# Scoring four attention units in one visit, w_out in longer rows, and earlier q and k requests, in a fused sliding-window attention and gated feed-forward kernel

## The chip, the cores and the metric

The kernel runs on one core of a Trainium2 chip. A core has a matrix engine (TensorE, here PE, with its weight loads shown apart as PEld), a vector engine (VectorE, DVE), a scalar engine (ScalarE, ACT), a general engine (GpSimd, POOL) and a synchronising engine (SyncE, SP). Each runs its own instruction stream in order; streams wait for each other on semaphores. Sixteen DMA engines move data between the chip's memory and the on-chip memories. Matrix products land in PSUM, eight banks of 512 float32 values in each of 128 partitions. The metric is the time of one execution in microseconds (us).

## What is computed

Sliding-window attention with sinks, and a two-layer feed-forward with a gate behind it, cut to what matters:

```python
B, H, S, D = 4, 8, 768, 64
scores = q @ k.T / sqrt(D)                    # per batch and head
keep = (key < 4) | ((0 <= query - key) & (query - key < 128))
a = softmax(where(keep, scores, -1e9))
x = (a @ v).transpose(0, 2, 1, 3).reshape(3072, 512)
h = x @ w_in                                  # (512, 2048)
g = h * sigmoid(beta * h)                     # beta has one value per hidden column
out = g @ w_out                               # (2048, 512), float32 out
```

The products are made from bfloat16 operands and summed in float32.

## The kernel before

The 3,072 tokens are cut into NT = 8 tiles of TT = 384 (half a sequence). A **unit** is one head pair in one token tile: 8 tiles x 4 pairs = 32 units, numbered so that units 4T to 4T+3 make token tile T. A unit with half = 1 (second half of a sequence) also needs scores against the four sink keys.

A unit goes through these steps. *In*: PE transposes its q and k (`transpose_in`, L626) and DVE or ACT copies them to `qkT`. *Sink*, *a*, *b*: scores. *Av*: the product with v (`attend`, L745) and the normalising on DVE (`normalise`, L776). *Out*: PE transposes the result (`transpose_out`, L786) and DVE copies it to `xT`. Units from XBAR = 12 on have both transposes made by DMA instead, and are scored in one visit: `scores_at_once` (L717) fills all four score banks (s0, s1, "tr", "av"), with one exponential and one mask of 1,536 columns a partition. Units 4 to 11 are scored in two half visits (`scores`, L680: steps a and b), each with two banks, an exponential (L707) and a mask (L714) of 768 columns. In these units the bank "tr" takes the transposes, "av" the value products.

The feed-forward has a first product per **block**: a block is one of NM = 16 groups of 128 hidden columns for one token tile, four matmuls of 128x384 (L814, `hidden_matmul`), then ACT's tanh (L822) and DVE's gate (L835). Banks h0 and h1 take turns; in token tile 0 the two accumulators help. The second product (`project`, L841) has 48 matmuls of 128x512 a token tile (3 token rows of 128 by 16 hidden groups) in the accumulators acc0 and acc1. For token tile 0 the order is rows 0 and 1 in turn, one in each accumulator, then row 2; later tiles go row by row.

A main loop (L938) over steps s writes the program in its natural order: at s = 0 to 15 the blocks of token tile 0; then a **gap** of eight steps (16 to 23) without blocks, in which units 4 to 7 are done; then the blocks of the other tiles. The table `AGENDA` says in which step each unit does what (units 8 to 11 begin at steps 23, 26, 28 and 31), and `products(s)` (L70) how many products of the second kind a step takes: three in the gap, two at steps 24 and 25, one to step 39, three from step 40. From this list a planner in the kernel (`Prog.order`, L184) builds each engine's real order before anything runs: it walks the operations with estimated durations and transfer times, and on each engine takes the ready operation that can start first, the earlier in the program where two are equal, within a window of 200 operations. So the order on an engine is fixed when the kernel is built, and at run time an engine waits for its next instruction even if a later one could go.

Transfers: SP requests q and k of units 0 to 11 (float32, `load_qk`, L517); POOL casts them (L621), makes masks, and requests w_in (four transfers, L578), w_out (eight transfers of two groups, L583), v of later tiles, and from unit 12 on the q, k and v (L552, L561). POOL's requests convert to bfloat16 on the way. An `after` argument makes a request wait for an earlier transfer's landing: q and k of units 4 to 7 wait for w_in's second transfer, `("w_in", 0, 4)`; those of units 8 to 11 for one of w_out's.

w_out's group m holds rows 128m to 128m+127, one row a partition, so a transfer of two groups reads two rows of 2 KB for each partition. Accordingly block m uses the hidden columns 128m to 128m+127 of w_in, and beta, which is read as 16 rows of 128 and transposed by PE (L883), gets one column a block.

Of the kernel before, what the change touches and what calls it, by code (L numbers as in the profile page):

```python
# [11 lines left out]
DM, DF, NOUT = 512, 2048, 512  # L12
NTOK = B * S
# [31 lines left out]

NEG = -1.0e6
# [10 lines left out]
for n in range(4, 8):  # L57
    for step, at in (("in", n - 4), ("sink", 16), ("a", 16), ("b", 16), ("av", 17), ("out", 18)):
        AGENDA.setdefault(at if step == "in" else at + 1 * (n - 4), []).append((n, step))
# [10 lines left out]
def products(s):  # L70

    return 0 if s < NM else 3 if s < NM + GAP or s >= 2 * NM + GAP else 2 if s < NM + GAP + 2 else 1
# [284 lines left out]
def bass_streamingllm_window__then__act_swish_beta_kernel(  # L357
# [32 lines left out]
    beta_stage = sb("beta_stage", (16, 128), F32)  # L390
# [183 lines left out]
    w_out_src = moe_w_out.rearrange("(m p) n -> p m n", p=128)  # L574
# [7 lines left out]
    def load_w_out(m, ms, after=()):  # L582
        op("gp", lambda e: e.dma_start(w_out16[:, m:m + ms, :], w_out_src[:, m:m + ms, :]), after=after,  # L583
           w=[("w_out", mm) for mm in range(m, m + ms)],
           dma=f"wo{m}", **transfer(ms * 128 * NOUT * 4, 416, 740.0, 3.0))
# [39 lines left out]

    def transpose_in(n, eng="dve"):  # L626
        _, _, half, pb = place(n)
        bank16 = tr_ps[:, :].bitcast(BF16)
        z = n % NQK
        for which, name in enumerate("qk"):  # L630
            with P.together("pe"):
                for c in range(3):
                    at = (3 * which + c) * 128
                    op("pe", lambda e, which=which, c=c, at=at: nc.tensor.transpose(
                        bank16[:, at:at + 128],
                        qk16[z][:, which, c, :, :].rearrange("p h d -> p (h d)"), ident[:, :]),
                       r=[(name + "16", z), "ident"], w=["tr"], **pe(128))
# [3 lines left out]
        op(eng, lambda e: (e.copy if eng == "act" else e.tensor_copy)(dst, src),  # L641
           x=["tr"], w=[("qkT", pb, half)], **(act(768) if eng == "act" else dve(865.0)))
# [168 lines left out]
    def hidden_matmul(i, c):  # L811
        T, m = i // NM, i % NM
        bank, name = hidden_bank(i)
        op("pe", lambda e: e.matmul(  # L814
            bank, w_in16[:, c, m * 128:(m + 1) * 128], xT[:, c, T * TT:(T + 1) * TT],
            start=(c == 0), stop=(c == 3)),
           r=[("w_in", c, m), ("xT", T, c)], w=[name], **pe(TT))
# [46 lines left out]
    op("act", lambda e: e.dma_start(beta_stage[:, :], moe_beta.rearrange("(m p) -> m p", p=128)),  # L864
# [4 lines left out]
    for c in range(6):  # L869
# [13 lines left out]
    op("pe", lambda e: nc.tensor.transpose(acc[1][:, 0:16], beta_stage[:, :], ident32[0:16, 0:16]),  # L883
       r=["beta_stage", "ident32"], w=["acc1"], **pe(64))
    op("dve", lambda e: e.tensor_scalar(beta_half[:, :], acc[1][:, 0:16], 0.5, None, ALU.mult),
# [15 lines left out]
    for n in range(4):  # L901
# [36 lines left out]
    for s in range(-2, S_END + NM):  # L938
# [4 lines left out]
        for n, step in AGENDA.get(s, ()):  # L943
# [5 lines left out]
            if step == "b" and n >= XBAR:  # L949
                scores_at_once(n)  # L950
                later.append(lambda n=n: mask_at_once(n))
            if step in ("a", "b") and n < XBAR:
                c = "ab".index(step)
                if n < 8 and c == 1:
# [86 lines left out]
```

## Time and profile before

| | |
|---|---|
| median of three runs | 229.1 us (228.0 to 230.09) |
| profiled execution | 228.59 us |
| its span, first to last instruction | 226.9 us |
| instructions | 4,463 |
| HBM read, written | 27.34 MB, 6.29 MB |

The profile shows one execution. "Busy" is time in which an engine executes, not counting its requests; a share is of the span. For PE, busy includes the time that a matmul takes to run through the array, which overlaps the next one, so what a matmul costs in a dense stream is the distance to the next start. PEclk is the clock that PE was granted, 1.00 being full. The chain of waits is followed back from the last instruction: at each step to what released it, or to the instruction before it on its engine. A row with `<-` names what ended an idle time. q0 is the DMA queue of POOL's requests, q1 that of SP's, q10 that of ACT's. "To landing" is the time from a request's issue to the arrival of its last byte.

### The profile page before, as it was taken

The numbers are of one execution on the slowest core, as the hardware profiler recorded it, in microseconds if no ns is written. First come the engines' busy times: TensorE is split into PE (matmuls) and PEld (weight loads), VectorE is DVE, ScalarE is ACT, GpSimd is POOL, SyncE is SP. The second block draws the span as 40 slices with busy tenths as digits, with TensorE's granted clock in tenths as the row PEclk, the third lists the DMA queues.
The fourth block names the chain that finished last, engine by engine and source line by source line (L and its number), as shares of the span: only waits on it lengthen the run. The fifth ranks groups of instructions, "written<-read, shape, count | busy, mean of one in ns | idle before, by whom it ended". The sixth has DMA issues, their size and how long they took to land.

```text
span 226.9 us, 4463 instructions
## 1 busy us (share of the span) xinstructions
PE 220.0 (97%) x1761; PEld 122.1 (54%) x1761; DVE 132.6 (58%) x264; ACT 141.3 (62%) x224; POOL 125.7 (55%) x191
## 2 busy tenths in 40 slices
PE   7999989999999999999999999999999999999995
PEld 4665545555555555555555555555555555555454
DVE  5466777488975776566565656555656564443200
ACT  1877796197586877566657766666656755555311
POOL 4689992899994979695939396876300000000000
PEclk9999999999999999999999999999999999999999
DMA  6999999999998999999999999998921012110122
GB/s 172 251 172 179 276 194 205 257 228 139 118 138 124 124 117 151 120 167 144 116 113 135 99 138 147 96 165 119 94 80 53 20 57 64 49 46 0 58 83 92
DMA packets 96901, 28.92 MB, mean 127 GB/s; under 512 B 83424, under 2 KB 93936, under 8 KB 96880
## 3 DMA queue, kind: packets, MB, share of 16 engines
q0 software_dynamic: 59232, 10.92, 65.7%
q1 hardware_dynamic: 34304, 16.79, 34.3%
q10 hardware_dynamic: 3344, 0.93, 1.9%
q8 instruction: 14, 0.23, 0.5%
q14 instruction: 7, 0.06, 0.1%
HBM read 27.34 MB, written 6.29 MB: 148 GB/s over the span
## 4 chain that ended last, share of the span: by engine, by line
PE 73%; DMA 15%; POOL 8%; issue 2%; SPq 1%; ACT 0%; POOLq 0%; ACTq 0%
PE acc L843 32%; PE h_ps L814 29%; DMA k_stage<-in_k_dram 8%; DMA w_out<-in_moe_w_out_dram 4%; PE s_ps L727 4%; PE s_ps L770 4%; POOL qk L621 3%; DMA w_in<-in_moe_w_in_dram 2%; POOL land L552 2%; PE h_ps L843 2%; POOL v_aug L561 1%; PE s_ps L759 1%; PE s_ps L670 1%; SPq L522 1%; POOL v_aug L532 0%
## 5 line engine op out<-in xcount | busy, mean ns | idle before, releaser
L822 ACT ACTIVATE th<-h_ps,beta_half 128x384 f32<-128x384 f32 x120 | 69.4, 581 | 59.7 <-PE h_ps L814 59.1
L843 PE MATMUL acc<-w_out,g 128*128 128x512 bf16 x368 | 99.7, 380 | 0.0
L814 PE MATMUL h_ps<-xT,w_in 128*128 128x384 bf16 x480 | 96.2, 326 | 0.0
L835 DVE SCALAR_TENSOR_TENSOR g<-th,h_ps 128x384 bf16<-128x384 f32 x120 | 65.6, 550 | 44.8 <-ACT th L822 44.0
L814 PEld LDWEIGHTS h_ps<-xT,w_in 128*128 128x128 bf16 x480 | 45.6, 98 | 39.8 <-issue 0.8
L843 PEld LDWEIGHTS acc<-w_out,g 128*128 128x128 bf16 x368 | 32.8, 98 | 28.8 <-issue 3.6
L552 POOL DMA_DIRECT2D land<-in_q_dram x40 | 30.2, 760 | 24.0 <-DVE rden L779 24.0
L552 POOL DMA_DIRECT2D land<-in_k_dram x40 | 30.3, 761 | 0.0
L561 POOL DMA_DIRECT2D v_aug<-in_v_dram x40 | 30.2, 760 | 0.0
L735 ACT ACTIVATE E<-s_ps 128x1536 bf16<-128x1536 f32 x20 | 28.8, 1442 | 0.0
L741 DVE TENSOR_TENSOR E<-E,mask 128x1536 bf16<-128x1536 bf16 x20 | 19.2, 958 | 16.4 <-ACT E L735 16.4
L851 ACT ACTIVATE out_sb<-acc 128x512 f32<-128x512 f32 x23 | 13.7, 596 | 7.6 <-PE acc L843 7.4
L770 PEld LDWEIGHTS s_ps<-v_aug,E 128*128 128x128 bf16 x336 | 15.2, 97 | 3.2 <-issue 1.2
L770 PE MATMUL s_ps<-v_aug,E 128*128 128x65 bf16 x336 | 16.8, 193 | 0.0
L707 ACT ACTIVATE E<-s_ps 128x768 bf16<-128x768 f32 x17 | 13.7, 811 | 4.3 <-PE s_ps L700 4.2
L781 DVE TENSOR_TENSOR o_norm<-s_ps,rden 128x384 bf16<-128x384 f32 x28 | 15.6, 556 | 0.8
L714 DVE TENSOR_TENSOR E<-E,mask 128x768 bf16<-128x768 bf16 x16 | 9.0, 572 | 2.0 <-ACT E L707 1.3
L727 PE MATMUL s_ps<-qkT 64*128 64x256 bf16 (+2 forms) x144 | 10.1, 254 | 0.0
L759 PE MATMUL s_ps<-v_sink,E_sink 128*128 128x130 bf16 x48 | 9.3, 219 | 0.0
L621 POOL CAST qk<-k_stage 128x384 bf16<-128x384 f32 x12 | 6.5, 544 | 4.7 <-DMA k_stage<-in_k_dram 4.4
L673 ACT ACTIVATE E_sink<-s_ps 128x384 bf16<-128x384 f32 x16 | 7.8, 490 | 1.5 <-PE s_ps L670 1.5
L727 PEld LDWEIGHTS s_ps<-qkT 64*128 64x128 bf16 x144 | 4.9, 94 | 7.1 <-issue 5.8
(75 smaller groups left out, 155.2 us busy)
## 6 DMA issues: line engine op xcount, KB each, us to landing
out_dram<-out_sb SPq DMA_DIRECT2D x23, 256.0 KB, 2.7
q_stage<-in_q_dram SPq DMA_DIRECT2D x12, 192.0 KB, 7.4
k_stage<-in_k_dram SPq DMA_DIRECT2D x12, 192.0 KB, 7.9
w_in<-in_moe_w_in_dram POOLq DMA_DIRECT2D x4, 512.0 KB, 6.8
w_out<-in_moe_w_out_dram POOLq DMA_DIRECT2D x8, 256.0 KB, 9.6
land<-in_q_dram POOLq DMA_DIRECT2D x40, 48.0 KB, 3.7
land<-in_k_dram POOLq DMA_DIRECT2D x40, 48.0 KB, 4.0
v_aug<-in_v_dram POOLq DMA_DIRECT2D x40, 48.0 KB, 3.4
```

The costliest lines, as they stand in the source:

```text
L552: op("gp", lambda e, d=d, s=s: e.dma_start(d, s), w=[("land", pb, half, x, hh)], after=after, dma=f"l{pb}{half}{x}{hh}", **transfer(TT * D ...
L561: op("gp", lambda e, d=d, s=s: e.dma_start(d, s), w=[("v", pb, 3 * half + c, hh) for c in range(3)], after=after, dma=f"lv{pb}{half}{hh}", ...
L707: op("act", lambda e: e.activation(both, src[:, :, 0:TT], AF.Exp, bias=0.0, scale=SCALE), x=list(names), w=[("E", n % NE, c)], **act(768))
L727: op("pe", lambda e, at=at, w=w, kb=kb, qb=qb, nq=nq, hh=hh, rows=rows, bank=bank: e.matmul(s_ps[:, 2 * hh + bank, at:at + w], keys_of(pb, ...
L735: op("act", lambda e: e.activation(E[z][:, :, :], src, AF.Exp, bias=0.0, scale=SCALE), x=list(S_NAMES), w=[("E", z, 0), ("E", z, 1)], **ac ...
L741: op("dve", lambda e: e.tensor_tensor(E[z][:, :, :], E[z][:, :, :], m.unsqueeze(1).to_broadcast([128, 2, 768]), ALU.mult), r=[("E", z, 0), ...
L770: last=(x == len(kbs) - 1): e.matmul(av_ps[:, at + hh * D1:at + hh * D1 + D1], E[z][:, hh, col:col + 128], v_aug[:, pb, hh, kb, 0:D1], sta ...
L781: op("dve", lambda e: e.tensor_tensor(o_norm[o][:, :, :, :].rearrange("p m h d -> p (m h) d"), src[:, :, 0:D], rden[z][:, :].unsqueeze(2). ...
L814: op("pe", lambda e: e.matmul(bank, w_in16[:, c, m * 128:(m + 1) * 128], xT[:, c, T * TT:(T + 1) * TT], start=(c == 0), stop=(c == 3)), r= ...
L822: op("act", lambda e: e.activation(th[i % 3][:, :], bank, AF.Tanh, bias=0.0, scale=beta_half[:, m:m + 1]), x=[name], r=["beta"], w=[("th", ...
L835: op("dve", lambda e: e.scalar_tensor_tensor(g[T % 2][:, m, :], th[i % 3][:, :], 1.0, bank, ALU.add, ALU.mult), r=[("th", i % 3)], x=[name ...
L843: op("pe", lambda e: e.matmul(bank[:, 0:width], g[T % 2][:, m, t * 128:(t + 1) * 128], w_out16[:, m, cols], start=(m == 0), stop=(m == NM ...
```

## The change

Units from ONCE = 8 on, not from 12 on, are scored in one visit over the four score banks. These banks are then not free for units 8 to 11's other steps, so a new function `aside` gives them another: unit 8's *in* keeps "tr"; the *in* of units 9 to 11, and *av* and *out* of units 8 to 11, go to acc1. To have acc1 free, the gap takes four products a step, which finishes rows 0 and 1 of token tile 0 by step 23, and steps 24 to 39 take one each, all of row 2 in acc0. The normalising of units 8 to 11 is written ahead of the step's gate rather than behind it.

w_out is read with four consecutive rows a partition: group m = 4g + j holds rows 512g + 4p + j. A transfer of two groups reads one run of 4 KB for each partition. Block m therefore uses every fourth column of w_in from 512g + j on (a step of four elements in the weights of L814), and beta is read as four rows of 512 and transposed in four pieces.

The requests of q and k for units 4 to 7 wait for w_in's first transfer, not its second. The first w_out request is written ahead of three v requests, not behind them.

```diff
+PER = 4
+ONCE = 8
 def products(s):
-    return 0 if s < NM else 3 if s < NM + GAP or s >= 2 * NM + GAP else 2 if s < NM + GAP + 2 else 1
+    return 0 if s < NM else 4 if s < NM + GAP else 3 if s >= 2 * NM + GAP else 1
...
-    beta_stage = sb("beta_stage", (16, 128), F32)
+    beta_stage = sb("beta_stage", (NM // PER, 128 * PER), F32)
...
-    w_out_src = moe_w_out.rearrange("(m p) n -> p m n", p=128)
+    w_out_src = moe_w_out.rearrange("(g p j) n -> p g j n", p=128, j=PER)
...
     def load_w_out(m, ms, after=()):
-        op("gp", lambda e: e.dma_start(w_out16[:, m:m + ms, :], w_out_src[:, m:m + ms, :]), after=after,
+        op("gp", lambda e: e.dma_start(w_out16[:, m:m + ms, :].rearrange("p j n -> p (j n)"),
+                                         w_out_src[:, m // PER, m % PER:m % PER + ms, :].rearrange("p j n -> p (j n)")), after=after,
...
+    def aside(n, step):
+        if n < 8:
+            return (av_ps, "av") if step == "av" else (tr_ps, "tr")
+        if n < XBAR:
+            return (tr_ps, "tr") if (n, step) in ((8, "in"),) else (acc[1], "acc1")
+        return (s_ps[:, 0, :], "s0") if step == "sink" else (av_ps, "av")
+
     def transpose_in(n, eng="dve"):
-        bank16 = tr_ps[:, :].bitcast(BF16)
+        bank, tr = aside(n, "in")
+        bank16 = bank[:, :].bitcast(BF16)
...
-            bank, w_in16[:, c, m * 128:(m + 1) * 128], xT[:, c, T * TT:(T + 1) * TT],
+            bank, w_in16[:, c, m // PER * 512 + m % PER:m // PER * 512 + 512:PER], xT[:, c, T * TT:(T + 1) * TT],
...
-    op("pe", lambda e: nc.tensor.transpose(acc[1][:, 0:16], beta_stage[:, :], ident32[0:16, 0:16]),
-       r=["beta_stage", "ident32"], w=["acc1"], **pe(64))
+    with P.together("pe"):
+        for j in range(PER):
+            op("pe", lambda e, j=j: nc.tensor.transpose(
+                acc[1][:, j * (NM // PER):(j + 1) * (NM // PER)], beta_stage[:, j:128 * PER:PER],
+                ident32[0:NM // PER, 0:NM // PER]),
+               r=["beta_stage", "ident32"], w=["acc1"], **pe(64))
...
                 for x in range(2):
-                    load_qk(y, x, [("w_in", 0, 4)])
+                    load_qk(y, x, [("w_in", 0, 0)])
...
             load_sinks(0, [("v", 3, 0, 0)])
+            load_w_out(0, 2, [("v", 3, 0, 0)])
             for c in range(3):
                 load_v(1, c, [("v", 3, 0, 0)])
-            load_w_out(0, 2, [("v", 3, 0, 0)])
...
-            if step == "b" and n >= XBAR:
+            if step == "b" and n >= ONCE:
                 scores_at_once(n)
                 later.append(lambda n=n: mask_at_once(n))
-            if step in ("a", "b") and n < XBAR:
+            if step in ("a", "b") and n < ONCE:
...
             if step == "av":
-                attend(n)
-                later.append(lambda n=n: normalise(n))
+                bank = aside(n, "av")
+                attend(n, *bank)
+                if ONCE <= n < XBAR:
+                    normalise(n, *bank)
+                else:
+                    later.append(lambda n=n, bank=bank: normalise(n, *bank))
...
             if step == "out" and n < XBAR:
-                transpose_out(n)
+                transpose_out(n, *aside(n, "out"))
```

More of the change, by code (lines that the diff above doesn't have):

```diff
@@ L58 @@
     for step, at in (("in", n - 4), ("sink", 16), ("a", 16), ("b", 16), ("av", 17), ("out", 18)):
-        AGENDA.setdefault(at if step == "in" else at + 1 * (n - 4), []).append((n, step))
+        AGENDA.setdefault(at if step == "in" else at + n - 4, []).append((n, step))
 for n in range(8, NU):
@@ L641, in transpose_in @@
         op(eng, lambda e: (e.copy if eng == "act" else e.tensor_copy)(dst, src),
-           x=["tr"], w=[("qkT", pb, half)], **(act(768) if eng == "act" else dve(865.0)))
+           x=[tr], w=[("qkT", pb, half)], **(act(768) if eng == "act" else dve(865.0)))
     def transpose_first(n):
```

10 lines of the change are left out of this document (6 added, 4 removed).

## The prediction

> **What bounds the kernel now.** I began with the page's engine line, then asked for busy time by stage, then read the chain of waits in order of time.
>
> ```profile
> PE 220.0 (97%) x1761; PEld 122.1 (54%) x1761; DVE 132.6 (58%) x264; ACT 141.3 (62%) x224; POOL 125.7 (55%) x191
> ...
> 17.30:28.90 11.60, 11.19 (x73) 6.38 (x72) 8.59 (x16) 8.70 (x17) 11.48 (x25) 1.00 1.19 228
> 28.90:35.10 6.20, 4.89 (x62) 2.54 (x60) 4.90 (x10) 6.13 (x11) 5.50 (x10) 1.00 1.64 193
> 35.10:44.50 9.40, 9.40 (x97) 5.43 (x96) 5.91 (x15) 3.67 (x6) 4.89 (x7) 1.00 1.25 234
> 44.50:66.80 22.30, 21.64 (x191) 12.09 (x189) 18.57 (x38) 16.33 (x27) 21.86 (x32) 1.00 1.68 159
> 66.80:211.20 144.40, 144.40 (x1095) 78.28 (x1095) 83.26 (x157) 93.67 (x145) 70.78 (x94) 1.00 0.96 103
> ```
>
> The stage rows give, after the length, the busy time of PE, PEld, DVE, ACT and POOL, then the granted clock (1.00 throughout) and the DMA share. From 66.8 us on PE never stops, and the change leaves that work alone: three products a block before and after, and every product is still made once. So the end moves by what PE gains or loses before 66.8 us. There it has three kinds of stage: the first hidden tile (to 28.9), whose blocks need w_in; the start of the gap (28.9 to 35.1), where ACT is busy 6.13 of 6.20 us and PE is not; and the second hidden tile (from 44.5), where POOL is busy 21.86 of 22.30 us. The chain shows what feeds them (start, length, work):
>
> ```profile
> 8.78 0.94 POOL w_in L578
> ...
> 12.45 5.50 DMA w_in<-in_moe_w_in_dram
> ...
> 17.96 0.37 SPq L522
> ...
> 58.58 0.53 POOL qk L621
> ...
> 61.38 0.17 PE s_ps L798 x3
> 61.55 0.27 PE s_ps L700 x2
> 61.82 0.76 PE h_ps L814 x4
> 62.96 0.27 PE s_ps L700 x4
> 65.23 0.37 PE s_ps L770 x12
> 65.60 0.65 PE h_ps L814 x4
> 66.25 0.65 PE acc L843 x3
> 66.90 0.44 PE s_ps L727 x8
> ```
>
> These PE pieces are times to the next start, so they are slots: a hidden block takes 0.65 us (0.163 a matmul), a product 0.65/3 = 0.217, a set of three transposes 0.17, a half visit of scores 0.27 and a whole visit 0.44. The piece ahead of a score visit reads 0.76 for 0.65: each visit pays another 0.1 us for the turn to 64-row mode.
>
> **The visits of units 8-11.** Each unit gives up two half visits, 2 x (0.27 + 0.1) = 0.74 us, for one whole visit, 0.44 + 0.1 = 0.54. Four units: **-0.8 us** of PE time. ACT and DVE also save a little (two exponentials become one, two masks one), which I cost at nothing: neither ends the chain there.
>
> **Requests of q and k for units 4-7.** They now wait for the first w_in transfer instead of the second.
>
> ```profile
> w_in<-in_moe_w_in_dram POOLq DMA_DIRECT2D x1, 512.0 KB, 5.7
> w_in<-in_moe_w_in_dram POOLq DMA_DIRECT2D x1, 512.0 KB, 9.8
> 15.57 0.74 POOL L578 DMA_DIRECT2D w_in<-in_moe_w_in_dram  x1 [0.30 <-POOL v_aug L532]
> PEld acc L814 <- DMA w_in<-in_moe_w_in_dram: 0.5, 1, 0.5
> q0 software_dynamic: 335, 0.34, 109.5%
> q1 hardware_dynamic: 866, 0.63, 90.7%
> ```
>
> The first two rows are the w_in requests at 8.78 and 15.57 us with their time to landing: they landed at 14.5 and 25.4. So q and k leave SP, which is L522 in the chain, some 3.5 us earlier than at 17.96 (the second w_in landed at 12.45 + 5.50), ahead of the last w_in request rather than behind all of them. PE already waited 0.5 us for that last transfer. The queue rows (packets, MB, share of the DMA engines) are for 18-20 and 25.4-28 us. From 18 to 20 POOL's queue (q0) moves alone although q and k were requested at 17.96: requests are served roughly in the order in which they came. Alone, a q or k load of 0.19 MB takes 0.19/0.63 x 2.6 x 0.907 = 0.7 us. SP has nothing else to issue then, so nothing waits behind them there. Two or three of the eight would be requested before the last w_in, so it lands about 1.5 to 2 us later. Bounds: nothing, if w_in stays ahead; 8 x 0.7 = 5.6 us, if all eight pass it. Part is covered: unit 4's keys land earlier too, and its transposes (two sets, 0.34 us) and the wait for its cast (0.29, the row at 26.78 below) move into this hole. I take **+0.6 us**, bounds 0 and +5. [...]
>
> **The gap, with w_out ahead of the v loads and four products a step.** First a wait of PE from the end of the first tile; then what PE does in 28.9 to 35.05, grouped by line; then POOL's v requests and the first w_out request behind them:
>
> ```profile
> 26.78 0.34 PE L634 MATMUL s_ps<-ident,qk 128*128 128x128 bf16 x3 [0.29 <-POOL qk L621]
> ...
> L634 PE MATMUL s_ps<-ident,qk 128*128 128x128 bf16 x18 | 1.8, 222 | 0.6 <-ACT qkT L641 0.4 <-DVE qkT L641 0.2
> L700 PE MATMUL h_ps<-qkT 64*128 64x128 bf16 (+1 forms) x16 | 1.6, 249 | 0.6 <-ACT E L707 0.6
> L700 PE MATMUL s_ps<-qkT 64*128 64x128 bf16 (+1 forms) x8 | 0.7, 248 | 0.1
> L770 PE MATMUL s_ps<-v_aug,E 128*128 128x65 bf16 x12 | 0.7, 194 | 0.0
> ...
> 22.20 2.68 POOL L542 DMA_DIRECT2D v_aug<-in_v_dram  x3
> w_out<-in_moe_w_out_dram POOLq DMA_DIRECT2D x1, 256.0 KB, 10.0
> ```
>
> By slots, this stretch held 18 transposes (1.0 us), 24 score matmuls in six half visits (2.2) and one unit's twelve value matmuls (0.4): 3.6 of 6.15 us, some 4 with the sinks, so about 2 us in which PE had nothing, since no product can start before the first w_out (requested at 24.9, landed 10.0 us later, at 34.9). The change puts this request ahead of the three v requests, which take POOL 2.68 us, and the transfers follow the requests; I expect it about 2.7 us earlier, at 32. That lets PE make four products (two m, two t) in the hole, 4 x 0.217 = 0.87 us. Units 4 and 5 arrive earlier by the two loads or so that pass w_in (0.7 us each), and ACT copies unit 5's keys before the crowded stretch. I take **-1.5 us**, bounds 0 (the earlier work only lengthens a later wait) and -2.0. What is late next is v for unit 4, by the one transfer that passes it (1.3 us or so, below); PE has products then. The larger number of products a step costs nothing in itself: six products of token tile 0 move from after 66.8 us to before it.
>
> **w_out in 4 KB rows.** The w_out requests and PE's waits for them:
>
> ```profile
> L583 POOL DMA_DIRECT2D w_out<-in_moe_w_out_dram x8: 700/706/736, 24.8 to 33.8; - x8
> DMA to landing us min/median/max: 8.9/9.6/11.3
> PEld acc L843 <- DMA w_out<-in_moe_w_out_dram: 0.2, 1, 0.2
> ...
> L814 PEld LDWEIGHTS h_ps<-xT,w_in 128*128 128x128 bf16 x480 | 45.6, 98 | 39.8 <-issue 0.8
> ```
>
> The last request goes out at 33.8; with the longest landing, 11.3, it is there at 45.1, so the eight follow each other by (45.1 - 34.9)/7 = 1.46 us, with other loads between. If time goes with bytes, longer rows change nothing; if with packets, it halves. PE's weight loads waited 0.2 us for w_out in all, so speed there is worth 0.2 at most. Against it, the gap now wants all 32 products of two token rows by its end (44.5), and the last transfer lands 0.6 us past it; a hidden block can go first. I put **0**, bounds -0.2 and +0.6. Price of the new layout: each hidden weight load steps over four elements. It lasts 98 ns beside a matmul slot of 163, so it hides unless it grows by two thirds: **0**. [...] The four beta transposes instead of one, and the smaller beta transfer, fall before 5 us, where the chain runs through k's first load and POOL: 0.
>
> **Eleven steps in one bank.** Units 9-11's key transposes and all four units' values and output transposes leave the two score banks for one accumulator, and PE is in order: a step issued before the bank is emptied holds the hidden blocks behind it, and ACT's tanh and DVE's gate behind those. The normalising of units 8-11 also goes ahead of the block's gate in the program, to empty the bank early, so that a gate can start 0.76 us later. DVE empties the bank:
>
> ```profile
> 59.53 0.96 DVE L641 COPY qkT<-s_ps 128x768 bf16<-128x768 bf16 x1
> 60.99 0.20 DVE L779 RECIPROCAL rden<-s_ps 128x6 f32<-128x6 f32 x1
> 61.22 0.56 DVE L781 TENSOR_TENSOR o_norm<-s_ps,rden 128x384 bf16<-128x384 f32 x1
> 61.69 0.35 DVE L802 COPY xT<-s_ps 128x384 bf16<-128x384 bf16 x1
> 59.16 0.34 PE L634 MATMUL s_ps<-ident,qk 128*128 128x128 bf16 x3 [0.47 <-POOL qk L621]
> ```
>
> The bank is held for 3 x (0.34 + 0.96) + 4 x (0.37 + 0.76) + 4 x (0.17 + 0.35) = 10.5 us of the 22.3, before DVE's own queue. It fits, with some waits: **+0.3 us**, bounds 0 and 11 x 0.47 = +5.2, by the longest wait of this kind in the stage.
>
> **Sum.** -0.8 + 0.6 - 1.5 + 0.3 = -1.4 us on the profiled execution of 228.59 us (span 226.9): **227.2 us**. The median of the three runs, 229.1, lies 0.5 above that execution, within their spread. One per cent, 2.3 us, is about what a measurement of this kernel can tell from no change.
>
> **Rivals.** First, *POOL keeps the time* (0.20). It is full from 44.5 us, and unit 11's cast ends at 59.1 on the chain. If PE comes there earlier and only waits longer, what the gap saved (-1.5) is lost and the visits (-0.8) are left, less the w_in and bank terms' 0.9: about 0, 228.5 us. For it: the 0.47 us wait. Against: products stand ready as cover. Second, *the shared bank stalls PE* (0.10): eleven waits of 0.47 us give 228.59 - 1.7 + 5.2 = 232.1 us. It decides from 1.7/11 = 0.15 us a step; against it, the kernel's planner sees the bank and places steps accordingly. Third, *everything closes up* (0.15): the gap's 2.0 us, the visits' 0.8 and the waits for POOL (0.29 + 0.47) go, with the late w_in covered: 225.0 us. Fourth, *strided weight loads bind* (0.04): at twice 98 ns a hidden matmul takes 196 for 163, 480 x 33 ns = 16 us more, 243 us. Fifth, *q and k hold up w_in* (0.05): all eight loads pass it, and PE stands idle for 5 us of it: 228.59 - 2.0 + 5.0 = 231.6 us.
>
> **Numbers.** The forecast has 0.46, its own range 226.2 to 228.2. Under 226.8 (over 1% faster) lie the third rival and 0.21 of the forecast: 0.36. Over 231.4 lie the fourth, most of the second and half of the fifth: 0.15. The rest, 0.49, is within 1%. The range 224.6 to 229.9 leaves out the three slow rivals, 0.19.
>
> **What would show it.** In the profile after: units 8-11 with four whole visits; w_out's first landing near 32 us and products before 33; the last w_in at 26.5 to 27.5 with a PE wait beside it; PE's lost time from 28.9 to 35 near 0.5 us; waits on the shared bank under 0.15 us each; hidden matmuls still 163 ns apart. A hidden slot over 163 ns, or w_in landing near 30 us with an idle PE, would make the prediction wrong.

## The result: slower, and the profile after

| | before | after |
|---|---|---|
| median | 228.55 us (4 runs) | 232.54 us (4 runs, 231.45 to 232.85) |
| ratio to before, 95% interval | | 1.016 (1.013 to 1.019) |
| profiled execution, its span | 228.59, 226.9 us | 232.85, 231.1 us |

The forecast of 227.2 us, its range and its sign were wrong. In the kernel after, L583, L621, L634, L727, L814 and L843 have become L588, L627, L649, L742, L829 and L858. The page's engine line of after:

```profile
PE 219.7 (95%) x1763; PEld 130.3 (56%) x1763; DVE 132.1 (57%) x260; ACT 141.0 (61%) x220; POOL 123.8 (54%) x191
```

PE has as much work as before and 4.5 us more without any. A profile shows one execution, and executions of one kernel differ by up to 3 us, so a wait read below is that execution's and not a mean. Stages cut at the first hidden block of each token tile show where the time goes (length; busy time of PE, PEld, DVE, ACT, POOL; granted clock). Before, from tile 0 and the gap to the end of tile 3's stage:

```profile
17.30:44.50 27.20, 25.48 (x227) 14.35 (x226) 19.39 (x39) 18.50 (x32) 21.87 (x41) 1.00 1.32 222
44.50:70.50 26.00, 25.34 (x229) 14.21 (x228) 20.45 (x41) 18.84 (x30) 23.16 (x33) 1.00 1.62 158
70.50:92.20 21.70, 21.70 (x191) 11.97 (x189) 14.84 (x29) 15.77 (x24) 18.12 (x24) 1.00 1.25 125
92.20:117.10 24.90, 24.90 (x193) 13.34 (x192) 14.88 (x29) 16.54 (x25) 18.13 (x24) 1.00 1.54 135
```

After, with a row of its own for the hole ahead of tile 1:

```profile
19.90:47.60 27.70, 25.91 (x232) 15.62 (x229) 19.20 (x39) 18.70 (x33) 17.27 (x36) 1.00 1.30 226
47.60:50.60 3.00, 0.54 (x7) 0.36 (x8) 0.00 (x0) 0.88 (x2) 3.00 (x5) 1.00 1.51 249
50.60:74.60 24.00, 24.00 (x225) 14.74 (x222) 19.64 (x37) 17.04 (x24) 21.39 (x31) 1.00 1.21 119
74.60:97.40 22.80, 22.80 (x190) 13.41 (x190) 15.49 (x30) 16.37 (x25) 18.13 (x24) 1.00 1.37 129
97.40:122.60 25.20, 24.50 (x190) 14.00 (x189) 14.63 (x29) 16.07 (x24) 18.13 (x24) 1.00 1.48 129
```

The stages don't hold equally many products: the orders put 28, 31, 31 and 48 of them into before's four, and 32, 31, 36 and 45 into after's. With 0.217 us taken off for each product more (and added for each fewer), after minus before is: start of the first tile +2.6, first tile and gap +2.7 (the hole of 47.6 to 50.4 is 2.5 of it), tile 1 -2.0, tile 2 0, tile 3 +0.9, the rest 0: +4.2 us in all.

So there are three losses. **The hole.** The chain of waits of after (start, length, work):

```profile
29.77 8.30 DMA w_out<-in_moe_w_out_dram
...
38.09 8.24 DMA q_stage<-in_q_dram
...
46.38 0.51 POOL qk L627
46.89 2.93 POOL land L557 x4
...
49.83 0.53 POOL qk L627
50.35 0.05 issue
50.40 0.34 PE s_ps L649 x3
```

POOL casts unit 8's q at 46.38, then issues four requests for unit 12, and only then casts its k. In before the four requests came ahead of both casts, which stood nearly side by side. POOL's timeline of before, from the second request on:

```profile
42.13 0.74 POOL L552 DMA_DIRECT2D land<-in_q_dram  x1
42.87 1.51 POOL L552 DMA_DIRECT2D land<-in_k_dram  x2
44.38 0.52 POOL L621 CAST qk<-q_stage 128x384 bf16<-128x384 f32 x1
45.31 0.51 POOL L621 CAST qk<-k_stage 128x384 bf16<-128x384 f32 x1 [0.42 <-DMA k_stage<-in_k_dram]
```

**Tile 3.** SP's timeline of after:

```profile
93.74 1.22 SPq L572 DMA_TRANSPOSE qkT<-land  x1
95.01 1.25 SPq L805 DMA_TRANSPOSE xT<-o_norm  x1
```

and DVE's:

```profile
92.40 0.56 DVE L796 TENSOR_TENSOR o_norm<-s_ps,rden 128x384 bf16<-128x384 f32 x1
```

Unit 15's result, the last piece of tile 3, is ready at 92.96, but its request stands behind unit 19's q and k transpose, which waits for its data to 93.7. In before, unit 15's comes first and the transpose that waits stands behind it:

```profile
87.10 1.19 SPq L790 DMA_TRANSPOSE xT<-o_norm  x1
88.33 0.58 SPq L859 DMA_DIRECT2D out_dram<-out_sb  x1
89.07 5.34 SPq L567 DMA_TRANSPOSE qkT<-land  x2
```

**The start.** ACT's timeline of before:

```profile
0.82 0.43 ACTq L864 DMA_DIRECT2D beta_stage<-in_moe_beta_dram  x1
1.28 3.37 ACTq L528 DMA_DIRECT2D v_stage<-in_v_dram  x6
4.68 1.28 ACT L871 ACT_TABLE_LOAD   x1 [4.68 <-issue]
```

and of after:

```profile
0.80 0.57 ACTq L879 DMA_DIRECT2D beta_stage<-in_moe_beta_dram  x1
1.40 4.98 ACTq L533 DMA_DIRECT2D v_stage<-in_v_dram  x6
6.41 1.28 ACT L886 ACT_TABLE_LOAD   x1 [6.41 <-issue]
```

Behind the four-row read of beta, the six v requests take 1.6 us longer to issue, so the table load and ACT's first copy come 1.7 us later. PE's waits of after (in all, number, longest) list all three places, and w_in:

```profile
PE s_ps L649 <- POOL qk L627: 2.5, 1, 2.5
PE s_ps L715 <- ACT qkT L674: 2.0, 1, 2.0
...
PE h_ps L829 <- DMA xT<-o_norm: 0.7, 1, 0.7
...
PE acc L829 <- DMA w_in<-in_moe_w_in_dram: 0.6, 1, 0.6
```

### The profile page after: what moved, and what is told of

The parts are those of the page before. It is cut to its first block, busy times and chain, and to the rows that moved or that the text cites. A ratio compares the mean times of both kernels' runs of the same rounds, so it can differ in the third digit from the quotient of the medians.

```text
span 231.1 us, 4464 instructions
## 1 busy us (share of the span) xinstructions
PE 219.7 (95%) x1763; PEld 130.3 (56%) x1763; DVE 132.1 (57%) x260; ACT 141.0 (61%) x220; POOL 123.8 (54%) x191
## 2 busy tenths in 40 slices
DMA packets 95853, 28.92 MB, mean 125 GB/s; under 512 B 83412, under 2 KB 91860, under 8 KB 95832
## 4 chain that ended last, share of the span: by engine, by line
PE 77%; DMA 10%; POOL 5%; ACTq 2%; ACT 2%; DVE 1%; issue 1%; SPq 1%; POOLq 0%
PE acc L858 30%; PE h_ps L829 30%; PE s_ps L742 4%; DMA w_out<-in_moe_w_out_dram 4%; DMA q_stage<-in_q_dram 4%; PE s_ps L785 3%; POOL land L557 2%; ACTq L533 2%; DMA land<-in_k_dram 2%; DMA xT<-o_norm 2%; PE h_ps L858 2%; POOL qk L627 1%; PE acc L785 1%; POOL v_aug L547 1%; PE acc L455 1%; PE acc L829 1%
## 5 line engine op out<-in xcount | busy, mean ns | idle before, releaser
L858 PE MATMUL acc<-w_out,g 128*128 128x512 bf16 x368 | 100.0, 380 | 0.4 <-DVE g L850 0.4
L829 PE MATMUL h_ps<-xT,w_in 128*128 128x384 bf16 x480 | 96.4, 326 | 0.7 <-DMA xT<-o_norm 0.7
L829 PEld LDWEIGHTS h_ps<-xT,w_in 128*128 128x128 bf16 x480 | 53.0, 114 | 35.3 <-DVE g L850 1.1
L858 PEld LDWEIGHTS acc<-w_out,g 128*128 128x128 bf16 x368 | 32.7, 98 | 27.6 <-issue 4.2
L750 ACT ACTIVATE E<-s_ps 128x1536 bf16<-128x1536 f32 x24 | 34.7, 1444 | 1.3 <-PE s_ps L742 1.2
L756 DVE TENSOR_TENSOR E<-E,mask 128x1536 bf16<-128x1536 bf16 x24 | 23.0, 957 | 15.6 <-ACT E L750 15.6
L566 POOL DMA_DIRECT2D v_aug<-in_v_dram x40 | 30.3, 761 | 0.0
L785 PEld LDWEIGHTS s_ps<-v_aug,E 128*128 128x128 bf16 x288 | 13.2, 97 | 3.0 <-issue 1.3
L785 PE MATMUL s_ps<-v_aug,E 128*128 128x65 bf16 x288 | 14.7, 193 | 0.0
L796 DVE TENSOR_TENSOR o_norm<-s_ps,rden 128x384 bf16<-128x384 f32 x24 | 13.3, 555 | 0.8
L742 PE MATMUL s_ps<-qkT 64*128 64x128 bf16 (+2 forms) x168 | 12.1, 257 | 0.0
L742 PEld LDWEIGHTS s_ps<-qkT 64*128 64x128 bf16 x168 | 5.7, 94 | 8.1 <-issue 6.1
L722 ACT ACTIVATE E<-s_ps 128x768 bf16<-128x768 f32 x9 | 7.2, 814 | 4.1 <-PE s_ps L715 4.1
L627 POOL CAST qk<-k_stage 128x384 bf16<-128x384 f32 x12 | 6.2, 514 | 5.7 <-DMA k_stage<-in_k_dram 5.7
L547 POOL DMA_DIRECT2D v_aug<-in_v_dram x6 | 5.4, 904 | 4.4 <-DMA w_out<-in_moe_w_out_dram 4.0
```

Source lines behind the costliest of these rows:

```text
L566: op("gp", lambda e, d=d, s=s: e.dma_start(d, s), w=[("v", pb, 3 * half + c, hh) for c in range(3)], after=after, dma=f"lv{pb}{half}{hh}", ...
L742: op("pe", lambda e, at=at, w=w, kb=kb, qb=qb, nq=nq, hh=hh, rows=rows, bank=bank: e.matmul(s_ps[:, 2 * hh + bank, at:at + w], keys_of(pb, ...
L750: op("act", lambda e: e.activation(E[z][:, :, :], src, AF.Exp, bias=0.0, scale=SCALE), x=list(S_NAMES), w=[("E", z, 0), ("E", z, 1)], **ac ...
L756: op("dve", lambda e: e.tensor_tensor(E[z][:, :, :], E[z][:, :, :], m.unsqueeze(1).to_broadcast([128, 2, 768]), ALU.mult), r=[("E", z, 0), ...
L785: last=(x == len(kbs) - 1): e.matmul(av_ps[:, at + hh * D1:at + hh * D1 + D1], E[z][:, hh, col:col + 128], v_aug[:, pb, hh, kb, 0:D1], sta ...
L796: op("dve", lambda e: e.tensor_tensor(o_norm[o][:, :, :, :].rearrange("p m h d -> p (m h) d"), src[:, :, 0:D], rden[z][:, :].unsqueeze(2). ...
```

## The experiments

Medians are of 12 runs (6 for the first, third and fourth kernel); before had medians of 228.7 to 228.95 beside them. Ratios are to before, with 95% intervals. Fillers are matmuls whose results are not used, which keep PE busy in a wait; the kernel before has some, and the rows with "fillers" have more. "Old layout" is w_out, w_in's columns and beta as in before; "late q and k requests" are those of units 4 to 7 behind the second w_in transfer again; "visits alone" is before with the visits, the shared bank and four products a step, and nothing else of the change.

| kernel | median, us | ratio |
|---|---|---|
| after, once more | 232.48 | 1.016 (1.012 to 1.020) |
| before, beta in four rows | 229.34 | 1.0026 (1.0005 to 1.0048) |
| after, unit 8's casts together | 230.53 | 1.010 (1.006 to 1.014) |
| after, old layout | 231.05 | 1.011 (1.009 to 1.014) |
| after, beta by POOL | 229.86 | 1.006 (1.004 to 1.008) |
| casts together, SP's order | 229.69 | 1.004 (1.001 to 1.007) |
| ... and fillers | 228.54 | 1.001 (0.999 to 1.003) |
| ... fillers, late q and k requests | 230.35 | 1.0065 (1.003 to 1.010) |
| casts, SP's order, beta by SP | 229.19 | 1.003 (1.0005 to 1.006) |
| ... beta by SP, late q and k requests | 228.84 | 1.0015 (0.999 to 1.004) |
| casts, SP's order, old layout | 228.36 | 0.999 (0.997 to 1.001) |
| ... old layout, late q and k requests | 227.92 | 0.997 (0.995 to 0.9995) |
| ... and fillers | 228.22 | 0.998 (0.995 to 1.001) |
| visits alone | 229.17 | 1.001 (0.9985 to 1.003) |
| visits alone, fillers | 228.67 | 1.000 (0.997 to 1.003) |
| before, fillers | 228.68 | 1.001 (0.998 to 1.004) |

### Each of the three places by itself

The changed kernel with unit 8's casts side by side; no other engine's order changes:

```diff
     def cast(n):
+        if n == 8 and P.group is None:
+            with P.together("gp"):
+                return cast(n)
```

> The changed kernel with one move on POOL: unit 8's cast of q stands behind the four requests for unit 12 and next to the cast of k, as before the change. Theory A (POOL waits for q of unit 8 with the four requests queued behind, and PE then waits 2.5 us for the cast of k): the 2.5 us wait falls under 1 us, and the kernel is faster by 1.6 to 2.5 us than the changed one, 230 to 231 us, with the late start still there. Theory B (q and k of unit 8 land too late in any order; POOL, full from then on, keeps the time): within 0.5 us of the changed kernel, 232.5 us.

Measured: 230.53 us, 2.0 under after, and no wait for a cast left. POOL's timeline of this kernel:

```profile
43.71 1.49 POOL L557 DMA_DIRECT2D land<-in_q_dram  x2 [2.35 <-DVE rden L797]
45.20 1.51 POOL L557 DMA_DIRECT2D land<-in_k_dram  x2
46.71 0.52 POOL L630 CAST qk<-q_stage 128x384 bf16<-128x384 f32 x1
47.15 0.51 POOL L630 CAST qk<-k_stage 128x384 bf16<-128x384 f32 x1
```

The q cast is later than in after (46.71 for 46.38), the k cast 2.7 us earlier (47.15 for 49.83): theory A.

In addition, SP requests unit 15's result ahead of unit 19's transpose (a `seq` orders two requests without a wait):

```diff
-           w=[("qkT", pb, half)], dma=f"t{pb}{half}", busy=1300.0, lag=1300.0)
+           w=[("qkT", pb, half)], dma=f"t{pb}{half}", busy=1300.0, lag=1300.0, seq="sp" if n == 19 else None)
...
-                r=[("o_norm", z)], w=[("xT", T, hp)], dma=f"x{z}", busy=1190.0, lag=650.0)
+                r=[("o_norm", z)], w=[("xT", T, hp)], dma=f"x{z}", busy=1190.0, lag=650.0, seq="sp" if n == 15 else None)
```

> The changed kernel with unit 8's casts side by side, and in addition, on SP, the transpose of unit 15's result requested ahead of unit 19's q and k transpose, as in the kernel before. Theory A (in the changed kernel SP stands waiting for unit 19's data with unit 15's result behind it, and PE waits 0.9 to 1.3 us for that result at the start of token tile 3): that wait goes, and it is faster than the kernel with the casts alone (230.5 us) by 0.9 to 1.3 us: 229.3 to 229.7 us. Theory B (PE meets the lost time at another place, since unit 15's result is late in itself): within 0.4 us of 230.5 us.

Measured: 229.69 us, 0.84 less than with the casts alone; tile 3's stage is back at before's length (24.92 us after the correction for products, for 25.97 without this move), and PE's wait for xT (0.9 us in the kernel with the casts alone) has gone. SP's timeline:

```profile
90.99 1.18 SPq L808 DMA_TRANSPOSE xT<-o_norm  x1
92.33 1.21 SPq L572 DMA_TRANSPOSE qkT<-land  x1
```

The third place, beta's read, put into the kernel before:

```diff
-    beta_stage = sb("beta_stage", (16, 128), F32)
+    beta_stage = sb("beta_stage", (4, 512), F32)
...
-    op("act", lambda e: e.dma_start(beta_stage[:, :], moe_beta.rearrange("(m p) -> m p", p=128)),
+    op("act", lambda e: e.dma_start(beta_stage[:, :], moe_beta.rearrange("(g x) -> g x", x=512)),
```

> The kernel before with one thing of the change: beta is read as four rows of 512 (four partitions) and transposed in four pieces; everything else keeps its place. Theory A (this read, first on ACT's queue, holds up the six v requests behind it, and with them ACT's table load, which came at 6.41 us after the change and at 4.68 before): slower by 1.7 to 2.5 us than before, the table load near 6.4 us, the first hidden tile at 19 to 20 us instead of 17.3. Theory B (the late start of the profiled execution is chance, or comes from another part): within 0.5 us of before, table load near 4.7 us.

Measured: 229.34 us, 0.5 slower (0.1 to 1.1 by the interval): neither theory in full. The mechanism is A's, by ACT's timeline:

```profile
5.79 1.28 ACT L871 ACT_TABLE_LOAD   x1 [5.79 <-issue]
```

and the first tile starts at 20.0 us for 17.3. But of these 2.7 us, 0.8 are won back in the first tile and the gap, and 0.7 in tile 1, whose two waits for POOL's casts (0.35 and 0.63 us lost at 50.2 and 58.5 in before) are gone. ("Lost" is the distance to the next start beyond the usual slot; the idle time that a timeline shows is some 0.16 us less.) So a late start is covered in part, because what follows had waits of its own.

### The layout

The changed kernel with w_out, the hidden blocks and beta in the old layout (that part of the diff taken back):

> The changed kernel with the old layout: w_out in 2 KB rows, hidden blocks of 128 adjacent columns, beta as 16 rows of 128. All orders but beta's stay those of the changed kernel, so the split cast of unit 8 stays. Theory A (beta's read costs the start, the longer rows and the strided weights cost nothing): faster than the changed kernel by 1.7 to 2.5 us, 230 to 231 us, the first hidden tile at 17.3 us, hidden matmuls 163 ns apart as in the changed kernel. Theory B (the start is chance): within 0.5 us of the changed kernel. Theory C (the longer rows speed up w_out): the first tile starts earlier, but q and k of unit 8, which wait for w_out's landings, come later, and less than 1 us is gained.

Measured: 231.05 us, 1.4 under after. The first tile starts at 17.7, but PE then has waits that after doesn't have, 0.7 us for a cast of POOL at 26.6 and 0.9 us for w_out, and 1.3 us instead of 0.7 for unit 15's result; so theory A's mechanism with a smaller gain. The strides cost no time: from tile 4 on, the stages of after, of this kernel and of before agree within 0.15 us. The load itself takes longer, though by less than the two thirds that the prediction allowed it: a strided weight load (after's row) takes 114 ns for 98, and hides beside a matmul slot of 163:

```profile
L829 PEld LDWEIGHTS h_ps<-xT,w_in 128*128 128x128 bf16 x480 | 53.0, 114 | 35.3 <-DVE g L850 1.1
```

The old layout, the casts side by side and SP's order of before, together:

> The changed kernel with the old layout, with unit 8's casts side by side and with SP's order of the kernel before: what stays is the visits, four products a step, the shared bank, the early q and k requests and w_out ahead of v. Theory A (the three places add up): 231.05 - 1.4 (PE's wait for the cast in the old layout) - 1.3 = 228.3 us, about the time of before. Theory B (POOL keeps the time whatever PE gains): no better than 230 us. Theory C (the gains forecast for the visits and the gap are there in full): 227 us.

Measured: 228.36 us, theory A's 228.3, closer than the interval of half a microsecond to either side can tell: the three places make up the whole loss, the layout taken as one. To find what in the layout costs, beta's read is requested by POOL instead:

```diff
-    op("act", lambda e: e.dma_start(beta_stage[:, :], ...
+    op("gp", lambda e: e.dma_start(beta_stage[:, :], ...
```

> The changed kernel with beta's read requested by POOL at its start instead of by ACT; the order built for POOL then also has unit 8's casts side by side. Theory A: both losses go, faster than the changed kernel by 3.5 to 5 us, 227.5 to 229 us. If only the start counts, 230 to 231; if neither counts, 232.5.

Measured: 229.86 us, 2.6 under after, less than expected: the tile still starts at 19.3, where PE waits 0.9 us for masks that POOL makes later, and tile 3 still loses 1.4. Beta's read requested by SP behind unit 0's loads, in the kernel with casts and SP's order mended:

> The changed kernel with unit 8's casts side by side and unit 15's result ahead of unit 19's transpose (229.7 us), and beta's four-row read requested by SP behind unit 0's two loads instead of first by ACT. Theory A (beta's place ahead of ACT's v requests is all that the new layout costs): ACT's table load near 4.3 to 4.8 us instead of 6.2, and 1.0 to 1.4 us faster, 228.4 us, the time of the same kernel with the old layout. Theory B (the 4 KB rows or the strided weights cost it): 229.7 us still, or hidden matmuls further apart than 163 ns.

Measured: 229.19 us, 0.5 less by the medians, with intervals that overlap; the table load at 4.82, the tile at 19.18. SP's later loads of q and k come half a microsecond later instead, and PE waits 0.7 us for casts of q. So this run doesn't separate the place of beta's read from what it pushes back.

### Why the start is late: PE's rate

Seven fillers of the same shape stand in PE's program in the stretch of 8 to 11 us. PE's timeline of before:

```profile
8.56 0.55 PE L450 MATMUL acc<-ones 128*128 128x128 bf16 x7
```

and of the kernel with casts and SP's order mended:

```profile
10.63 0.95 PE L455 MATMUL acc<-ones 128*128 128x128 bf16 x7
```

Seven starts 56 ns apart, against seven 107 ns apart: PE runs at half rate there, while the clock column of the profile (the third number from the end) says 1.00, in the window of 10 to 12 us of the second kernel:

```profile
10.00:12.00 2.00, 2.00 (x14) 1.14 (x13) 1.48 (x3) 0.52 (x1) 2.00 (x4) 1.00 0.74 98
```

The clock column shows the half rate in this case's profiles only where PE had been at full rate before. In after the fillers stand 56 ns apart at 5.9 us; then PE waits 2.0 us for ACT's first copy, and the next stretch reads 0.50, with fillers 107 ns apart at 10.9:

```profile
4.73:8.14 3.41, 1.07 (x13) 0.73 (x13) 1.11 (x2) 1.72 (x3) 0.81 (x2) 1.00 1.09 282
8.14:11.56 3.42, 3.24 (x24) 2.07 (x24) 1.08 (x3) 2.02 (x4) 2.28 (x5) 0.50 0.87 212
```

In the row ahead of the fall PE was busy for 1.07 of its 3.41 us. In the kernel with casts and SP's order mended, where PE waits 1.7 us for ACT's first copy, fillers stand 107 ns apart from the first ones, at 1.2 us, to those at 11.2, and the column says 1.00 all that time. In before, where PE waits 0.2 us ahead of its first scores, they stand 107 ns apart at 5.8 us and 56 ns at 8.6. That the wait keeps PE at half rate was the author's estimate from these profiles, so sixteen more fillers fill the wait for ACT's first copy:

```diff
         placed = self.order()
+        first = next(i for i, n in enumerate(placed) if n.eng == "pe" and n.mode == 64)
+        for _ in range(16):
+            f = Node(-1, "pe")
+            f.items.append((self.filler[0], None, [self.filler[2]]))
+            placed.insert(first, f)
```

> The changed kernel with unit 8's casts side by side and unit 15's result ahead of unit 19's transpose (229.7 us), and sixteen more filler matmuls of 128x128 on PE just ahead of the first scores, where PE waits 1.7 us for ACT's first copy; their results are not used. Theory A (the wait makes PE fall to, or stay at, half rate, where a filler takes 107 ns and not 56, until some 12 us, and this is most of the late start): fillers after 9 us take 56 ns, the first hidden tile starts at 18.5 to 19 us instead of 20.0, the time falls by 0.4 to 0.9 us. Theory B (ACT's late copy alone makes the late start): the tile starts at 20 us as before and the time stays within 0.3 us.

Measured: 228.54 us, 1.15 less than without the fillers, with the new layout kept and the table load still late (6.05 us). The seven fillers in PE's timeline of this kernel:

```profile
9.93 0.55 PE L460 MATMUL acc<-ones 128*128 128x128 bf16 x7
```

The tile starts at 18.98, 1.07 us earlier. That is theory A, and all but 0.2 us of what the old layout brought: most of the layout's price was PE's rate at the start. (The profiled execution took 229.66 us, 1.1 above its kernel's median, with 1.6 us of waits for w_in, so its span shows only 0.3 us of the gain.) It was not only the layout that could bring the half rate: the profile with beta's read on SP has it to 10.5 us, that with the read on POOL to 11.2, and one with the old layout, below, to 12.9.

Does the half rate also cost the kernel before? Eight fillers there:

> The kernel before with eight more filler matmuls on PE ahead of the first scores (results not used). Theory A (in some executions of the kernel before PE also stays at half rate until 12 us, and these make its spread of 227.6 to 230.1 us): the median falls by 0.2 to 0.6 us and the spread becomes narrower. Theory B (its spread has other causes): the median stays within 0.2 us or rises by the fillers' own 0.5 us.

Measured: 228.68 us, ratio 1.0007: no difference, spread 228.3 to 231.2. Theory B by the time: these fillers narrow nothing. What makes the spread is not shown, but the rate may have a part in it: of the 122 runs of before beside these kernels, 11 have a granted clock of 0.992 to 0.993, and their mean is 229.4 us, for 228.7 of the others.

### Where the forecast gains went

Visits, bank and four products a step alone, in the old layout and with the old requests:

> The kernel before with the visits, the shared bank and four products a step alone: old layout, q and k of units 4-7 behind the second w_in transfer, w_out behind the v loads. The order built for it has the casts of unit 8 side by side and unit 15's result ahead of unit 19's transpose. Theory A (the visits are worth their 0.8 us and the bank costs little): 228.0 us, 0.5 to 1 us faster than before. Theory B (POOL keeps the time): equal to before. Theory C (the shared bank stalls PE): slower by 1 us or more, with waits of PE beside the bank.

Measured: 229.17 us, ratio 1.001: theory B by the time. Its profiled execution was at half rate to 12.9 us (first tile at 19.5), so once more with eight fillers:

> The kernel before with the visits, the shared bank and four products a step alone, and the same eight filler matmuls, so that it starts as the kernel before with fillers does. Theory A (the visits' 0.8 us are there and the start hid them): 0.5 to 1.0 us faster than the kernel before with fillers. Theory B (POOL keeps the time, and what PE saves becomes waiting): within 0.3 us of it.

Measured: 228.67 us, the time of before with the same fillers: B again by the time. The stages of the profiled executions (first block to first block, corrected for products as above; "rest" is from tile 4 to the end of PE's work) don't show B's reason:

| us | start | first tile and gap | tile 1 | tile 2 | tile 3 | rest |
|---|---|---|---|---|---|---|
| before | 17.3 | 27.2 | 26.0 | 21.7 | 24.9 | 107.1 |
| before, fillers | 18.2 | 26.9 | 25.3 | 21.7 | 24.9 | 107.1 |
| visits | 19.5 | 26.7 | 24.8 | 21.8 | 24.9 | 107.1 |
| visits, fillers | 18.0 | 28.6 | 24.7 | 21.9 | 24.9 | 107.1 |
| after | 19.9 | 29.8 | 24.1 | 21.7 | 25.8 | 107.1 |
| casts, SP's order, fillers | 19.0 | 28.4 | 24.1 | 21.7 | 24.9 | 107.1 |
| casts, SP's order, old layout | 17.8 | 29.7 | 24.0 | 21.6 | 24.9 | 107.2 |
| ... late q and k requests | 17.8 | 27.2 | 24.5 | 21.6 | 24.9 | 107.1 |

The visits do shorten tile 1, by 0.6 us against before with fillers, and by 1.2 in the kernels whose rows say 24.1, and PE waits for no cast there. In the profile of the visits with fillers the gap takes more than that back: it is 1.75 us longer, of which PE's waits for the last w_in (0.77 lost) and for w_out (0.71) are most. Four products a step want every w_out transfer inside the gap; PE's timeline of the visits with fillers:

```profile
46.29 0.82 PE L862 MATMUL acc<-w_out,g 128*128 128x512 bf16 x3 [0.54 <-DMA w_out<-in_moe_w_out_dram]
```

The last w_out landed at 46.25. In before it lands at 45.07, and the gap's 28 products don't need it. But this execution took 229.62 us, 0.95 above its kernel's median: w_in and w_out landed 1.3 and 1.0 us later than in before with fillers (26.8 for 25.4, 46.3 for 45.3), though the edit touches no request of theirs. In the profile without fillers (229.22 us, at its median) there is no wait for either and the gap is not longer; there the late start is what takes the gain. So the visits' gain is real in tile 1 and reaches the end in neither, and where a typical execution loses it stays open.

The requests of q and k for units 4-7, put back behind the second w_in transfer, in the old layout:

```diff
-                    load_qk(y, x, [("w_in", 0, 0)])
+                    load_qk(y, x, [("w_in", 0, 4)])
```

> The kernel with the old layout, the casts side by side and SP's order mended (228.36 us), with q and k of units 4-7 behind the second w_in transfer again. Theory A (the early requests delay w_in, for which PE waited 2.9 us in that kernel's profile, where the start is early): these waits fall under 0.6 us and the time by 1 to 2 us, 226.4 to 227.4 us, below the kernel before. Theory B (what q and k gain in the gap is lost again, or POOL keeps the time): within 0.4 us of 228.4 us.

Measured: 227.92 us, 0.44 less: just beyond theory B's bound, far from A's, and with intervals that overlap. Among PE's waits in the kernel without this edit stood

```profile
PE acc L831 <- DMA w_in<-in_moe_w_in_dram: 2.9, 3, 1.5
```

and with it this wait is gone; but that profiled execution took 229.64 us, 1.3 above its kernel's median. Of the sixteen kernels here this is the only one whose interval lies below before, 0.3% (0.05 to 0.5), and one such interval among sixteen can be chance. The same move in two kernels with the new layout, first the one with fillers, then the one with beta's read on SP:

> The changed kernel with casts, SP's order and fillers mended (228.54 us), and with q and k of units 4-7 behind the second w_in transfer again. Theory A (the early requests cost the w_in waits that its profile shows, 1.6 us, and bring less): 0.5 to 1.5 us faster, 227.0 to 228.0. Theory B (the early requests cost and bring about the same in this layout): within 0.4 us of 228.54.

> The same as the kernel with beta's read on SP, with q and k of units 4-7 behind the second w_in transfer again. Theory A: both gains add up, 226.8 to 227.8 us. Theory B (q and k earlier or later makes no difference): the time of the kernel with beta's read on SP.

Measured: 230.35 us, 1.8 slower, and 228.84, 0.35 faster (228.54 and 229.19 without the move). Three kernels, two signs, and only the 1.8 us are clear of the spread. The move also changes POOL's order: in the kernel with fillers w_out's second request then stands ahead of unit 5's cast of q (at 28.92), without the move behind it (at 29.32). So the runs don't say whether the early requests in themselves pay; that stays open. The fastest kernel with the fillers added:

> The fastest kernel so far (old layout, casts and SP's order mended, q and k behind the second w_in transfer, w_out ahead of v, 227.92 us) with the eight filler matmuls. Theory A (its start is now and then at half rate): 227.3 to 227.7 us. Theory B (its start is always at full rate): 227.9 us, or up to 0.5 us more for the fillers.

Measured: 228.22 us, ratio 0.998: theory B. And the changed kernel itself, once more:

> The changed kernel once more, to stand beside the kernels that differ from it by one step: 232 to 233 us, with the 2.5 us wait of PE for unit 8's cast and the wait near 98 us for the last piece of token tile 3.

Measured: 232.48 us. PE's wait for unit 8's cast is 2.0 us here, that for unit 15's result only 0.2. But the hole costs twice in this execution, since half rate follows it:

```profile
46.52:49.93 3.41, 1.35 (x14) 0.64 (x12) 0.36 (x1) 1.09 (x2) 3.41 (x6) 1.00 1.46 252
49.93:53.34 3.41, 3.05 (x11) 1.27 (x12) 1.51 (x2) 1.12 (x2) 3.41 (x7) 0.50 1.69 228
```

A run of four hidden matmuls takes 1.30 us at 49.75, for 0.81 at 54.87, and tile 1 takes 25.7 us for the 24.1 of the first profile, where full rate followed the wait of 2.5 us. So in some executions the split casts cost more than the wait itself.

## Why the prediction was wrong

**The failed step: the orders of POOL and SP.** The prediction moved requests and took the rest of each engine's order from before, though it knew of the planner. That put two waits at nothing, and its premise that the work behind 66.8 us is left alone failed with it: one of the two comes at 97 us. The planner builds the order anew, by its own estimates of landings, and operations change places. Unit 8's cast of k fell behind four requests (2.0 us by the median), and unit 15's result behind a transpose that waits for data (0.8). The rival "POOL keeps the time" named the right kind of wait, but could at most take back what the gap and the visits saved (228.5 us), and its evidence was before's 0.47 us on unit 11; no rival had an order that changes. In the order that the planner makes for the changed kernel with the early requests of q and k alone, or with w_out ahead of v alone, the casts stay together; in that for before with these two moves and nothing else they do too. It takes both moves and the visits. For unit 15's result either move is enough. (These orders were not run.)

**"The four beta transposes instead of one, and the smaller beta transfer, fall before 5 us ... : 0."** Wrong: beta's read alone costs 0.5 us in before, and the layout as a whole 1.3 to 1.4 in the changed kernel, of which fillers give back 1.15. A short transfer was taken for a cheap one; it stood first on ACT's queue, and PE's first scores wait for ACT's first copy, which comes behind six requests and the table load. The prediction priced neither that wait nor PE's rate after it.

**The gap, -1.5.** Its first half came: w_out's first landing at 31.7, first product at 33.0 (32 and "before 33" forecast). The gain did not. With the hole taken out, first tile and gap are 27.3 us in after for 27.2 in before, the bound "nothing" of this term. The price of wanting all of w_out in the gap had stood under w_out with 0.6; it is 0.7 in the one profile that shows it. With the three losses gone (228.36 us, ratio 0.999) the forecast -1.4 us is not there either, but 0.2 by the ratio and 0.6 at most by its interval: of the 5.3 us between 227.2 and 232.5, the losses are 4.1 and the gains that didn't come about 1.2.

**Right, or right in kind.** The visits: -0.8 forecast, -0.6 to -1.2 in their stage, but not in the time of the whole. Early q and k: +0.6, and PE's wait for w_in in after's profile is 0.6; that the number is the same is luck, since the last w_in landed at 28.6, later than the 27.5 forecast, and profiles of other kernels with this move show waits from none to 2.9 us. The shared bank: +0.3 forecast, none seen (PE is busy for 24.00 of 24.00 us in tile 1). 4 KB rows and strided weights: 0 and 0 forecast, and 0 as far as the runs separate them. Of the signs named beforehand, whole visits, w_out's first landing, the bank's waits and the matmul distance of 163 ns held; PE's 0.4 us without work from 28.9 to 35 fits as well, but by luck, since the first tile's blocks now run there. The products came at 33.0 and the last w_in too late, and the sign for a wrong prediction, an idle PE beside w_in, was not the one that came.

## What to carry to other kernels

Where a planner or scheduler orders the queues, compare the new order with the old on every in-order engine before pricing a change: a wait that the edit doesn't touch can move ahead of something urgent. What a stage saves may not reach the end, as with the visits here; ask for each gain which transfer PE meets next. And look at the spacing of equal matmuls in the first microseconds and behind every long wait: with beta's longer-lasting read first on ACT's queue, PE was still at half rate at 11 us in all five profiles without added fillers, and sixteen filler matmuls in the wait gave back 1.15 us. That is no general remedy: eight fillers brought nothing in three other kernels.

## What the runs showed of the hardware that was not expected

Beta's read of 8 KB in four rows instead of sixteen, first on ACT's queue, went with a delay of the six requests behind it: ACT's table load came at 5.54 to 6.41 us in all seven profiles with it, and at 4.52 to 5.33 in the eleven without. Why is not shown; in after the last two of the six took 1.24 and 1.58 us each to issue, for 0.53 and 0.65. PE's half rate is visible in the spacing of equal matmuls (107 and 56 ns) where the clock column still says 1.00, which it does in these profiles until PE has first been at full rate. After that a fall shows: in after behind a stretch of 3.41 us in which PE was busy for 1.07, and in its repeat behind one with 1.35; each lasted 3.4 us. In after's hole none came, though PE was busy for only 0.93 of the 3.41 us from 46.98 to 50.39; what brings a fall is not shown. And w_out's requests in 4 KB rows take POOL 0.53 to 0.58 us each to issue, for 0.70 to 0.74 in 2 KB rows.
